# One small tile 128 bytes larger, and weight stores, loads, root steps, activations and result stores at other places in a fused attention and two-MoE kernel

## The chip, the cores and the metric

One core of a Trainium2 chip. The metric is the device time of one launch in microseconds (us): the median of the runs. Lower is better.

## What is computed

```python
kv  = einsum('bhsd,bhse->bhde', k, v)            # b=8, h=8, s=576, d=64
o   = einsum('bhsd,bhde->bhse', q, kv)
x   = o / sqrt(mean(o*o, -1) + 1e-6) * g_norm    # to (4608 tokens, 512)
h   = x @ moe_w_in;   x = (h * sigmoid(h)) @ moe_w_out      # 512 -> 2048 -> 512
h   = x @ moe2_w_in;  out = (s * relu(h)**2 + b) @ moe2_w_out
```

All tensors are fp32. The four weights are 512x2048 or 2048x512. Their product with 4608 tokens is nearly all of the arithmetic.

## The kernel before, in words

Every fp32 operand of the four large products is split into a high and a low part, and a product is three passes of matmuls (high by high, high by low, low by high). Attention and the first matrix (`emit_h`, L489) make up the **first stage**: 7 blocks of 512 tokens, each with 16 slots of 12 matmuls of 512 columns. Between the slots `attend` (L555) places the attention of the batches that come later. For batch b a table `UNITS` names the number of its 128-token tiles and the slot where it begins. One slot after another does `emit_qT` (transposes, tile `pq`), `out_tile` (`po`, the sum of squares, a copy), then the root of the mean by Newton steps on DVE (`rsqrt_steps`, 12 short operations that `run_between` takes in portions), `norm_tile`, and one `xT_tile` a slot (transposes into `px`, ACT writes `xh`, DVE writes `xl`, the two moving operands of a later block). `pq`, `po` and `px` share two PSUM banks. Tiles of batches that no block of the first stage takes are written to DRAM through a buffer `xs`.

Beside this, `weight_steps` (L203) re-codes the weights of the later stages: one call of `steps` does one small piece, and 2 or 3 are taken in a slot (3 in the second half of a block). `split` writes a piece into one half (a granule) of one of four rooms `SPARES`, and stores it to DRAM (`wd<-wo`) by a deferred call: `defer(n, f)` runs f after n slots.

The rest of the work uses Strassen-Winograd products, seven instead of eight, named P1, P5, P6, P2, P7, P4, P3 (k = 0 to 6 in this order): **hidden1** (the last 1024 tokens of the first MoE's first matrix, with SiLU of sums of two products, `add_square`), **out2** (the first MoE's second matrix), **hidden3** and **out4** (the same of the second MoE). out2, hidden3 and out4 take blocks b = 1 to 4 of 512 columns and last b = 0 with half as many. In hidden3 and hidden1 a group g is seven products of six matmuls, and four results `g` of a group are stored to DRAM (`Hidden.out`, `gt<-g`). With b = 0 each such store has 128 KB, the others 256 KB. Results rotate through rooms `G_ROOMS`, by `turn % 4` in hidden3's blocks 1 to 4, `turn % 7` otherwise. The output stages read them again (`Output.load`: `ka`, `r`, `sa`), and the re-coded weights (`grid.load`: `w<-wd`). A unit of an output stage is 24 matmuls, with one cast on ACT (L845) and one subtraction on DVE (L847) that write its moving operand `o`. out4 transposes its result (`rows_out`, `pt`), copies it to `out_c` or `out` in turn (ACT, L876) and stores it.

What sets the order: it is written out by hand, and each engine works through its own list in order. SP issues the loads and the stores of stages 2 and 3's weights; ACT issues the stores of `g`, `y` and the result, between its own operations. A DMA that has to wait holds everything behind it on that engine. SP and ACT draw on the same eight DMA semaphores in turn, so an issue also waits until the eighth DMA before it has landed.

Tiles live in "rooms" of fixed size that lie in SBUF one behind another, in the order of their first use. The tile `r` (L436, L1147: 4 x 5 x 8 floats a partition, 640 bytes) is first used after `wr_0`, `wr_1`, W4 to W6 and W8 to W11, and before all other rooms that PE reads in the large products. In the built kernel the first group starts at 32 modulo 256 bytes (288 modulo 512), the second at 160 modulo 256 (416 modulo 512). In the output stages the weights of product k, slice a are in W{4k+a} and the moving operand is in one of four rooms of the second group (`RING`, L577). In the hidden stages the weights are in W{k+7a}, and the moving operand is in the second group, but that of P6, which is in `wr_0`.

Of the kernel before, what the change touches and what calls it, by code (L numbers as in the profile page):

```python
# [8 lines left out]
F32 = mybir.dt.float32  # L9
# [8 lines left out]
def kernel(  # L18
# [36 lines left out]
    nc = tc.nc  # L55
# [77 lines left out]
    raw_t = {}  # L133
    wf_t = {}
# [68 lines left out]
    def weight_steps(stage, raws, sums_in, granule, slots, behind=None):  # L203
# [40 lines left out]
        def step(i, what):  # L244
            if i < NF:
                decode(stage, i, what)
                if what == "merge":
                    n = i + len(raws)
                    if n < NF:
                        load_raw(stage, n, raws[n % len(raws)])  # L250
                    elif behind:
                        load_raw(behind, n - NF, raws[n % len(raws)])

        def begin():
            if stage == 4:
                csum.append(room("gl_1", [P, T], F32, "csum"))
                nc.vector.memset(csum[0], 0.0)
            for i, tag in enumerate(raws):
                if (stage, i) not in raw_t:
                    load_raw(stage, i, tag)  # L260
# [172 lines left out]
    def out_tile(t):  # L433
        b, i = t
        if i == 0:
            r_t[b] = small.tile([P, 4, (TT + 1) * H], F32, tag="r", name=f"r{b}", bufs=1)  # L436
        ps = ps_a.tile([P, H, D], F32, tag="a", name=f"po{b}_{i}")
        emit_out(t, ps, range(NP))
        emit_squares(t, ps, r_t[b][:, 0, i * H:(i + 1) * H])
        xn_t[t] = xn_page(t)  # L440
        nc.scalar.copy(xn_t[t], ps)
# [113 lines left out]
    def attend(slot):  # L555

        for b, n, s in UNITS:
            d = slot - s
            lead = 4 if b == 1 else 6
            if 0 <= d + lead < n:  # L560
                load_q(b, d + lead)
            if 0 <= d < NP and b + 1 < B:
                load_kv(b + 1, d)
        for b, n, s in UNITS:
            d = slot - s
            if d == -2:
                emit_kv(b, range(NP))
            if 0 <= d < n:
                out_tile((b, d))
            if -1 <= d < n - 1:  # L570
                emit_qT((b, d + 1))
            if d == n - 1:
                between.extend(rsqrt_steps(r_t[b], n))
            if b > 1 and n - 1 <= d < n + 2:
                run_between(4)
            if d == n + 2:
                run_between(len(between))  # L577
                for i in range(2):
                    norm_tile((b, i))
            if d == n + 3:  # L580
                for i in range(2, n):
                    norm_tile((b, i))
            if n + 3 <= d < 2 * n + 3:
                xT_tile((b, d - n - 3))
# [9 lines left out]
    class Hidden:  # L594
# [5 lines left out]
        def __init__(self, stage, order):  # L600
            self.stage, self.order, self.gt = stage, order, gt[stage]
            self.raw, self.slots, self.banks, self.turn = {}, {}, {}, 0
            self.seq = [(b, i) for b in order for i in range(NF)]
# [112 lines left out]
        def out(self, g, f, h, slots):  # L716
            b = self.seq[g][0]
            self.turn += 1
            r = room(self.G_ROOMS[self.turn % (4 if b and self.stage == 3 else 7)], [P, T], F32, f"g{self.stage}_{b}_{f}_{h}")[:, :size[b]]
            defer(slots if b else slots + 1, lambda: nc.scalar.dma_start(self.gt[b][f, h], r))  # L720
            return r
# [9 lines left out]
        def add_square(self, g, f, h, x, y):  # L731
# [5 lines left out]
            if self.stage == 1:  # L737
                nc.scalar.activation(r, r, AF.Silu)
# [34 lines left out]
    class Output:  # L773


        def __init__(self, stage):
# [4 lines left out]
            self.turn = 0  # L781
            self.keep, self.t = {}, []
# [13 lines left out]
        def load(self, upto):  # L796
            while self.loaded < min(upto, len(self.units)):
                u = self.loaded
                self.loaded += 1
                b, k, a = self.units[u]  # L800
                n = size[b]
                if k == P1 and u < NA:
                    self.load_kept(b, a)
                if k in (P5, P2, P7):
                    x, h = int(k == P2), int(k != P2)
                    r = self.r[u] = pair(R_ROOMS[self.turn % 4], f"r{self.stage}_{u}")[:, :, :n]
                    self.turn += 1
                    nc.sync.dma_start(r, self.gt[b][4 * a + x:4 * a + 4:2, h].rearrange("i p t -> p i t"))
                if k == P6:
                    if a not in self.s:  # L810
                        self.s[a] = room(SPARES[a], [P, 2, T], F32, f"sa{self.stage}_{a}")
                    nc.sync.dma_start(
                        self.s[a][:, :, :n], self.gt[b][4 * a + 1:4 * a + 4:2, 1].rearrange("i p t -> p i t")
                    )
# [55 lines left out]
        def rows_out(self, b, h, r):  # L870
# [13 lines left out]
            def store():  # L884
                for part, rows in rows_of(*t):
                    nc.scalar.dma_start(rows, o[part])
# [188 lines left out]
    def beside1(b, i, k):  # L1075
# [4 lines left out]
        if i == 3 and k == P1:  # L1080
            out2.load(2)
        if i == NF - 1:
# [14 lines left out]
    def beside3(b, i, k):  # L1097
# [8 lines left out]
        if i == 3 and k == P1:  # L1106
            out4.load(2)
        if i == NF - 1:
# [11 lines left out]
    with tc.manual_schedule():  # L1120
# [26 lines left out]
        r = r_t[0] = small.tile([P, 4, (TT + 1) * H], F32, tag="r", name="r0", bufs=1)  # L1147
# [44 lines left out]
        def in_pages(n):  # L1192
# [3 lines left out]
            weight_steps(2, ("wr_0", "wr_1"), ("v_0", "v_1"), in_spares(), 1, behind=3),  # L1196
            weight_steps(3, ("wr_0", "wr_1"), ("v_0", "v_1"), in_spares(), 1),
# [44 lines left out]
```

## Time and profile before

| what | value |
|---|---|
| runs | 1593.0, 1596.1, 1598.49 us; median 1596.1 |
| profiled execution, its own time | 1598.04 us |
| its span in the trace | 1595.9 us |
| mean granted clock of TensorE | 0.992 of full speed |
| busy share: TensorE weight loads, DVE, ACT | 82%, 63%, 52% |
| HBM read, written | 211.81 MB, 140.51 MB |

The profiled execution is 1.9 us above the median. Times in the views count from the start of its span. PE is TensorE, PEld its weight loads; a name such as `py` or `o` is a tile of the program with its numbers left out; `a<-b` is written and read; L931 is a line of the kernel. The first stage lasts until 433 us, hidden1 until 511, out2 until 863, hidden3 until 1219, out4 until the end.

### The profile page before, as it was taken

What the parts mean: (1) busy time and instruction counts of PE and PEld (TensorE: products, weight loads), DVE (VectorE), ACT (ScalarE), POOL (GpSimd) and SP (SyncE); (2) the same over time, 40 slices, a digit from 0 to 9 for tenths busy, and PEclk for the clock granted to TensorE, in tenths of its full rate; (3) what the DMA queues carried; (4) which work ended last, traced back from release to release, by engine and by line L of the source; (5) the groups of instructions that cost most, each with busy time, mean ns of one, the idle gap of its engine ahead of it and who ended that gap; (6) DMA issues with size and microseconds to landing.
All of it is one profiled execution on the core that took longest, in us unless ns stands there. A gap on an engine that the chain in (4) does not pass through costs nothing.

```text
span 1595.9 us, 21844 instructions
## 1 busy us (share of the span) xinstructions
PE 1561.9 (98%) x8184; PEld 1305.3 (82%) x8184; DVE 1007.3 (63%) x1385; ACT 833.1 (52%) x1331; POOL 1.6 (0%) x8
## 2 busy tenths in 40 slices
PE   7999999999999999999999999999999999999998
PEld 5888788887887788888898788888889888888888
DVE  4645465456673958676767666666546757576745
ACT  3655545555454444444445565656555454546454
POOL 0000000000000000000000000000000000000000
PEclk8999999999999999999999999999999999999999
DMA  8978898977655982727259847475466872726241
GB/s 251 268 246 276 267 303 289 294 259 258 219 204 200 361 314 94 240 79 249 75 204 354 337 166 264 156 279 198 179 226 249 334 278 80 235 82 237 67 145 54
DMA packets 228937, 353.77 MB, mean 222 GB/s; under 512 B 56800, under 2 KB 96736, under 8 KB 228832
## 3 DMA queue, kind: packets, MB, share of 16 engines
q1 hardware_dynamic: 162176, 240.95, 45.5%
q10 hardware_dynamic: 66656, 111.44, 19.1%
q8 instruction: 64, 1.05, 0.3%
q14 instruction: 41, 0.34, 0.1%
HBM read 211.81 MB, written 140.51 MB: 221 GB/s over the span
## 4 chain that ended last, share of the span: by engine, by line
PE 88%; DMA 6%; ACT 2%; DVE 2%; issue 1%; ACTq 1%; SPq 0%; DVEq 0%
PE ph L495 19%; PE qy L931 18%; PE qv L931 11%; PE py L708 11%; PE qx L931 11%; PE px L708 7%; PE pv L708 7%; PE po L385 2%; DMA gt<-g 1%; PE pkv L351 1%; PE pq L375 1%; DMA r<-gt 1%; PE px L461 1%; PE pt L874 1%; DMA out_dram<-out 1%
## 5 line engine op out<-in xcount | busy, mean ns | idle before, releaser
L931 PE MATMUL qy<-o,w 128*128 128x512 f32 (+1 forms) x1440 | 301.6, 369 | 0.4 <-DVE o L847 0.4
L931 PEld LDWEIGHTS qy<-o,w 128*128 128x128 f32 x1440 | 251.7, 189 | 47.4 <-DVE o L847 0.6
L847 DVE TENSOR_TENSOR o<-ka,o 128x1024 fp32r<-128x1024 f32 (+1 forms) x160 | 178.5, 1116 | 127.5 <-ACT o L845 125.1
L845 ACT CAST o<-ka 128x1024 fp32r<-128x1024 f32 (+1 forms) x160 | 153.4, 963 | 166.2 <-PE qv L931 63.0
L931 PE MATMUL qv<-o,w 128*128 128x512 f32 (+1 forms) x960 | 207.6, 374 | 4.1 <-ACT o L845 2.9
L931 PE MATMUL qx<-o,w 128*128 128x512 f32 (+1 forms) x960 | 203.5, 369 | 2.4 <-ACT o L845 1.7
L931 PEld LDWEIGHTS qv<-o,w 128*128 128x128 f32 x960 | 169.5, 192 | 35.7 <-ACT o L845 3.1
L931 PEld LDWEIGHTS qx<-o,w 128*128 128x128 f32 x960 | 167.0, 189 | 32.9 <-ACT o L845 2.1
L708 PE MATMUL py<-x,w 128*128 128x512 f32 (+1 forms) x720 | 164.0, 372 | 4.5 <-ACT g L734 4.3
L708 PEld LDWEIGHTS py<-x,w 128*128 128x128 f32 x720 | 126.7, 189 | 30.2 <-ACT g L734 5.5
L502 ACT ACTIVATE g<-ph 128x512 f32<-128x512 f32 x112 | 67.0, 598 | 154.4 <-PE ph L495 152.0
L495 PE MATMUL ph<-xh,wh 128*128 128x512 f32 x448 | 128.1, 408 | 3.3 <-ACT xh L465 3.3
L845 ACT CAST o<-r 128x1024 fp32r<-128x1024 f32 (+1 forms) x80 | 77.1, 963 | 89.3 <-PE qy L931 44.7
L495 PE MATMUL ph<-xl,wh 128*128 128x512 f32 x448 | 121.3, 393 | 0.0
L495 PE MATMUL ph<-xh,wl 128*128 128x512 f32 x448 | 120.2, 390 | 0.0
L708 PE MATMUL pv<-x,w 128*128 128x512 f32 (+1 forms) x480 | 113.0, 371 | 0.0
L708 PE MATMUL px<-x,w 128*128 128x512 f32 (+1 forms) x480 | 112.8, 371 | 0.0
L847 DVE TENSOR_TENSOR o<-r,o 128x1024 fp32r<-128x1024 f32 (+1 forms) x80 | 89.4, 1118 | 36.0 <-ACT o L845 35.1
L495 PEld LDWEIGHTS ph<-xl,wh 128*128 128x128 f32 x448 | 84.6, 189 | 19.1 <-DVE xl L466 0.2
L495 PEld LDWEIGHTS ph<-xh,wl 128*128 128x128 f32 x448 | 84.4, 188 | 18.3
L708 PEld LDWEIGHTS px<-x,w 128*128 128x128 f32 x480 | 85.4, 190 | 15.8
L708 PEld LDWEIGHTS pv<-x,w 128*128 128x128 f32 x480 | 85.2, 190 | 16.0
(156 smaller groups left out, 1878.5 us busy)
## 6 DMA issues: line engine op xcount, KB each, us to landing
r<-gt SPq DMA_DIRECT2D x96, 512.0 KB, 5.2
w<-wd SPq DMA_DIRECT2D x84, 512.0 KB, 7.1
gt<-g ACTq DMA_DIRECT2D x160, 256.0 KB, 2.3
gt<-g ACTq DMA_DIRECT2D x56, 512.0 KB, 4.8
wd<-wo SPq DMA_DIRECT2D x112, 256.0 KB, 4.3
wr<-in_moe_w_in_dram SPq DMA_DIRECT2D x16, 1024.0 KB, 6.5
wr<-in_moe_w_out_dram SPq DMA_DIRECT2D x16, 1024.0 KB, 6.5
ka<-gt SPq DMA_DIRECT2D x32, 512.0 KB, 3.8
```

What stands on the lines that cost most here:

```text
L351: nc.tensor.matmul(ps[r, p, r], ka[:, i, d], va[:, i, d], start=(p == pairs[0] and c == 0), stop=False, skip_group_check=True,)
L375: nc.tensor.transpose(ps[:, p * P:(p + 1) * P], a[:, p * P:(p + 1) * P], ident)
L385: nc.tensor.matmul(po[off:off + n, p * P:(p + 1) * P], qT_t[t][:, p, off:off + n], kvw[b % 2][:, p, :], start=True, stop=True,)
L461: nc.tensor.transpose(ps[:, p, :], xn[:, p * P:(p + 1) * P], ident)
L495: nc.tensor.matmul(ps, wt[:, c, :], xt[:, c, :], start=(n == 0 and c == 0), stop=(n == 2 and c == KT - 1))
L502: nc.scalar.activation(both[:, i], ps, AF.Silu)
L708: nc.tensor.matmul(ps, a[s][c], x[t][c], start=(k in (P1, P5) and n == c == 0), stop=(n == 2 and c == 1), skip_group_check=True,)
L845: nc.scalar.copy(o[:, :, 0], x)
L847: nc.vector.tensor_sub(o[:, :, 1], x, o[:, :, 0])
L874: nc.tensor.transpose(ps[:, e * P:(e + 1) * P], self.c[b, h, e][:, r * P:(r + 1) * P], ident)
L931: nc.tensor.matmul(ps, t[:, s], self.o[u][:, i, p], start=(k in (P1, P5) and a == i == m == 0), stop=(a == NA - 1 and i == 1 and m == 2), ...
```

## The change

- `r` is given as 4 x 6 x 8 floats, 768 bytes. In the built kernel all rooms behind it start 128 bytes later: the second group is now at 32 modulo 256 (32 modulo 512), the first stays at 32 modulo 256 (288 modulo 512).
- Weight stores of stages 2 and 3 are deferred by three slots instead of one, and the load of a raw weight into a room that was just read is deferred too.
- `q` loads come 8 slots ahead instead of 6. The 12 root steps are taken as 6 and 6 instead of 4, 4, 4, and norm and transposes come one slot earlier.
- In hidden1, SiLU of a sum of two products is deferred by two slots.
- The first loads of out2 and out4 (`ka_0`, and the first four `r`) stand earlier, one by one (`fetch`).
- In the half block two results share one room and one store (`halves`).
- The result stores of the last two blocks (b = 4 and 0) are issued by SP.

```diff
@@ weight_steps, step and begin
                 if what == "merge":
                     n = i + len(raws)
-                    if n < NF:
-                        load_raw(stage, n, raws[n % len(raws)])
-                    elif behind:
-                        load_raw(behind, n - NF, raws[n % len(raws)])
+                    to, n, tag = stage, n, raws[n % len(raws)]
+                    if n >= NF:
+                        to, n = behind, n - NF
+                    if to:
+                        asked.add((to, n))
+                        defer(slots, lambda: load_raw(to, n, tag))
...
-                if (stage, i) not in raw_t:
+                if (stage, i) not in asked:
                     load_raw(stage, i, tag)
@@ out_tile (and the same for r0)
-            r_t[b] = small.tile([P, 4, (TT + 1) * H], F32, tag="r", name=f"r{b}", bufs=1)
+            r_t[b] = small.tile([P, 4, 6 * H], F32, tag="r", name=f"r{b}", bufs=1)
@@ attend
-            lead = 4 if b == 1 else 6
+            lead = 4 if b == 1 else 8
...
-            if b > 1 and n - 1 <= d < n + 2:
-                run_between(4)
-            if d == n + 2:
+            if b > 1 and n - 1 <= d < n + 1:
+                run_between(6)
+            if d == n + 1:
                 run_between(len(between))
                 for i in range(2):
                     norm_tile((b, i))
-            if d == n + 3:
+            if d == n + 2:
                 for i in range(2, n):
                     norm_tile((b, i))
-            if n + 3 <= d < 2 * n + 3:
-                xT_tile((b, d - n - 3))
+            if n + 2 <= d < 2 * n + 2:
+                xT_tile((b, d - n - 2))
@@ Hidden.out
-            b = self.seq[g][0]
-            self.turn += 1
-            r = room(self.G_ROOMS[self.turn % (4 if b and self.stage == 3 else 7)], [P, T], F32, f"g{self.stage}_{b}_{f}_{h}")[:, :size[b]]
-            defer(slots if b else slots + 1, lambda: nc.scalar.dma_start(self.gt[b][f, h], r))
-            return r
+            b, i = self.seq[g]
+            if b:
+                self.turn += 1
+                r = room(self.G_ROOMS[self.turn % (4 if self.stage == 3 else 7)], [P, T], F32, f"g{self.stage}_{b}_{f}_{h}")
+                defer(slots, lambda: nc.scalar.dma_start(self.gt[b][f, h], r))
+                return r
+            n = int(f % 2 != h)
+            if (g, n) not in self.halves:
+                self.turn += 1
+                t = self.halves[g, n] = room(self.G_ROOMS[self.turn % 7], [P, 2, size[b]], F32, f"g{self.stage}_{b}_{i}_{n}")
+            else:
+                t = self.halves[g, n]
+                rows = self.gt[b][2 * i:2 * i + 2].rearrange("f h p t -> p (f h) t")
+                rows = rows[:, 1:3] if n else rows[:, 0:4:3]
+                defer(slots, lambda: nc.scalar.dma_start(rows, t))
+            return t[:, f % 2]
@@ Hidden.add_square
-                nc.scalar.activation(r, r, AF.Silu)
+                defer(2, lambda: nc.scalar.activation(r, r, AF.Silu))
@@ Output: load is cut in two, fetch(u) does what its body did, once for a unit
+                self.fetch(self.loaded - 1)
+        def fetch(self, u):
+            if u in self.fetched:
+                return
+            self.fetched.add(u)
...
@@ Output.rows_out
-                    nc.scalar.dma_start(rows, o[part])
+                    (nc.sync if b in order[-2:] else nc.scalar).dma_start(rows, o[part])
@@ beside1
-        if i == 3 and k == P1:
+        if i == 1 and k == P6:
             out2.load(2)
+        if i in (2, 3, 4, 5) and k == P2:
+            out2.fetch(NA + i - 2)
@@ beside3
-        if i == 3 and k == P1:
+        if i == 1 and k == P1:
             out4.load(2)
+        if i in (1, 2, 3, 4) and k == P2:
+            out4.fetch(NA + i - 1)
@@ the call of weight_steps for stages 2 and 3
-            weight_steps(2, ("wr_0", "wr_1"), ("v_0", "v_1"), in_spares(), 1, behind=3),
-            weight_steps(3, ("wr_0", "wr_1"), ("v_0", "v_1"), in_spares(), 1),
+            weight_steps(2, ("wr_0", "wr_1"), ("v_0", "v_1"), in_spares(), 3, behind=3),
+            weight_steps(3, ("wr_0", "wr_1"), ("v_0", "v_1"), in_spares(), 3),
```

**PE, end of the first block of the first stage.** `px_0` to `px_4` are batch 1's transposes, `ph_15` is the block's last slot and `ph_0` the next block's first. Before:

```order
L461 MATMUL px_2_908<-ident,xnp_71 128x128 x4
L495 MATMUL ph_15_920<-xh_406,wh_806 128x512 x4
L495 MATMUL ph_15_920<-xl_407,wh_806 128x512 x4
L495 MATMUL ph_15_920<-xh_406,wl_826 128x512 x4
L461 MATMUL px_3_935<-ident,xnp_71 128x128 x4
L495 MATMUL ph_0_949<-xh_863,wh_230 128x512 x4
L495 MATMUL ph_0_949<-xl_864,wh_230 128x512 x4
L495 MATMUL ph_0_949<-xh_863,wl_232 128x512 x4
L461 MATMUL px_4_966<-ident,xr_765 128x128 x4
```

and now:

```order
L464 MATMUL px_2_891<-ident,xnp_71 128x128 x4
L498 MATMUL ph_14_900<-xh_406,wh_806 128x512 x4
L498 MATMUL ph_14_900<-xl_407,wh_806 128x512 x4
L498 MATMUL ph_14_900<-xh_406,wl_837 128x512 x4
L464 MATMUL px_3_916<-ident,xnp_71 128x128 x4
L498 MATMUL ph_15_926<-xh_406,wh_806 128x512 x4
L498 MATMUL ph_15_926<-xl_407,wh_806 128x512 x4
L498 MATMUL ph_15_926<-xh_406,wl_837 128x512 x4
L464 MATMUL px_4_940<-ident,xr_765 128x128 x4
L498 MATMUL ph_0_954<-xh_848,wh_230 128x512 x4
```

The transposes `px_0` to `px_3`, from which the second block's operands are made, stand one slot earlier: between the last of them and the block's first matmul there is now a whole slot, and `px_4`, a tile that the block does not read.

**SP, end of hidden1 and start of out2** (`w` are weights of out2, `ka` and `r` its first inputs, `sa` later ones). Before:

```order
L315 DMA w_0_0_4303<-wd_0_0_75 128x1024
L792 DMA ka_0_4382<-gt_1_161 128x2x512 x2
L315 DMA w_0_1_4395<-wd_0_1_76 128x1024
L315 DMA w_0_2_4482<-wd_0_2_77 128x1024
L315 DMA w_0_3_4567<-wd_0_3_78 128x1024
L315 DMA w_1_0_4640<-wd_1_0_79 128x1024
L315 DMA w_1_1_4708<-wd_1_1_80 128x1024
L792 DMA ka_1_4727<-gt_1_161 128x2x512 x2
L808 DMA r_4_4782<-gt_1_161 128x2x512
L808 DMA r_5_4784<-gt_1_161 128x2x512
L808 DMA r_6_4786<-gt_1_161 128x2x512
```

and now:

```order
L808 DMA ka_0_4245<-gt_1_161 128x2x512 x2
L318 DMA w_0_0_4306<-wd_0_0_75 128x1024
L829 DMA r_4_4353<-gt_1_161 128x2x512
L318 DMA w_0_1_4397<-wd_0_1_76 128x1024
L829 DMA r_5_4445<-gt_1_161 128x2x512
L318 DMA w_0_2_4486<-wd_0_2_77 128x1024
L829 DMA r_6_4534<-gt_1_161 128x2x512
L318 DMA w_0_3_4573<-wd_0_3_78 128x1024
L829 DMA r_7_4617<-gt_1_161 128x2x512
L318 DMA w_1_0_4648<-wd_1_0_79 128x1024
L318 DMA w_1_1_4716<-wd_1_1_80 128x1024
L808 DMA ka_1_4735<-gt_1_161 128x2x512 x2
```

The first `ka` and four `r` now alternate with the loads of weights, each of which waits for its room; only the second `ka` still stands in the last stretch.

**ACT, half block of hidden3** (`g_0_...` are results, `gt_0` their stores). Before:

```order
L728 ACTIVATE g_0_4_0_10166<-px_10112 128x256
L729 ACTIVATE g_0_4_0_10166<-g_0_4_0_10166 128x256
L734 COPY g_0_5_1_10175<-py_10119 128x256
L753 COPY py_10186<-px_10179 128x256
L720 DMA gt_0_165<-g_0_2_1_10156 128x256
L720 DMA gt_0_165<-g_0_4_0_10166 128x256
L728 ACTIVATE g_0_5_0_10208<-py_10119 128x256
L729 ACTIVATE g_0_5_0_10208<-g_0_5_0_10208 128x256
L720 DMA gt_0_165<-g_0_5_1_10175 128x256
L758 COPY u_10218<-py_10186 128x256
L720 DMA gt_0_165<-g_0_5_0_10208 128x256
```

and now:

```order
L773 COPY u_10212<-py_10185 128x256
L743 ACTIVATE g_0_3_0_10228<-px_10178 128x256
L744 ACTIVATE g_0_3_0_10228<-g_0_3_0_10228 128x256
L749 COPY g_0_3_0_10228<-py_10185 128x256
L735 DMA gt_0_165<-g_0_2_1_10203 128x2x256
L768 COPY py_10250<-px_10243 128x256
L735 DMA gt_0_165<-g_0_3_0_10228 128x2x256
L743 ACTIVATE g_0_3_1_10268<-py_10185 128x256
L744 ACTIVATE g_0_3_1_10268<-g_0_3_1_10268 128x256
```

A group has two stores of two results each where it had four of one, and a room comes round again after 7 stores, which are now three and a half groups, where they were one and three quarters.

## Rows read from the trace of the kernel before

**Rows 1.** Page, part 1: busy time, share of the span, number of instructions.
```profile
PE 1561.9 (98%) x8184; PEld 1305.3 (82%) x8184; DVE 1007.3 (63%) x1385; ACT 833.1 (52%) x1331; POOL 1.6 (0%) x8
```

**Rows 2.** Windows: length, busy us (count) by engine; then PEclk, DMA share, GB/s.
```profile
1170.00:1220.00 50.00, 45.70 (x351) 44.39 (x350) 21.27 (x43) 25.72 (x65) 0.00 (x0) 0.97 0.59 202
...
1540.00:1596.00 56.00, 47.30 (x368) 46.17 (x367) 29.51 (x48) 27.17 (x49) 0.00 (x0) 0.92 0.26 76
```

**Rows 3.** Waits of PE, whole span: total us, times, longest us.
```profile
PE py L708 <- ACT g L734: 5.0, 4, 2.6
PE ph L495 <- ACT xh L465: 3.3, 4, 0.8
...
PE pq L375 <- DVE xl L466: 1.5, 2, 0.8
```

**Rows 4.** Chain in order of time, stages 2 and 3: start us, us, what.
```profile
591.14 10.89 PE qx L931 x48
602.02 11.09 PE qv L931 x48
613.12 11.15 PE qy L931 x48
...
1018.36 2.75 PE py L708 x12
...
1095.39 2.75 PE py L708 x12
```

**Rows 5.** The same chain in the first stage, end of its first block.
```profile
89.26 2.75 PE ph L495 x12
...
92.44 2.76 PE ph L495 x12
```

**Rows 6.** Waits of SP, 168 to 181 us, first stage.
```profile
SPq L240 <- DVE wo L238: 9.4, 3, 5.2
```

**Rows 7.** Timeline of PE, start of the second stage; in brackets idle before, and releaser.
```profile
508.40 1.20 PE L708 MATMUL py<-x,wh 128*128 128x512 f32 x4 [0.67 <-ACT g L734]
...
518.55 0.50 PE L931 MATMUL qx<-o,w 128*128 128x512 f32 x1 [1.69 <-ACT o L845]
519.81 1.45 PE L931 MATMUL qx<-o,w 128*128 128x512 f32 x5 [0.76 <-DVE o L847]
```

**Rows 8.** Timeline of ACT, the same stretch.
```profile
517.45 1.99 ACT L845 CAST o<-ka 128x1024 fp32r<-128x1024 f32 x2 [3.85 <-DMA gt<-g]
```

**Rows 9.** Timeline of PE, half block of the third stage.
```profile
1178.74 1.70 PE L708 MATMUL py<-x,w 128*128 128x256 f32 x12 [1.25 <-ACT g L734]
...
1186.60 2.10 PE L708 MATMUL py<-x,w 128*128 128x256 f32 x12 [2.59 <-ACT g L734]
```

**Rows 10.** Timeline of ACT, the same stretch.
```profile
1173.97 0.33 ACTq L720 DMA_DIRECT2D gt<-g  x1
...
1185.45 0.38 ACT L728 ACTIVATE g<-px 128x256 f32<-128x256 f32 x1 [4.47 <-DMA gt<-g]
```

**Rows 11.** Windows of 2 us, the same stretch, columns as in rows 2.
```profile
1188.00:1190.00 2.00, 2.00 (x12) 2.00 (x11) 0.00 (x0) 0.79 (x2) 0.00 (x0) 0.50 0.93 289
1190.00:1192.00 2.00, 2.00 (x15) 2.00 (x14) 0.85 (x2) 0.71 (x3) 0.00 (x0) 0.74 0.89 275
```

**Rows 12.** Timeline of PE, start of the last half block.
```profile
1547.29 3.00 PE L931 MATMUL qv<-o,w 128*128 128x256 f32 x24
1553.23 6.00 PE L931 MATMUL qv<-o,w 128*128 128x256 f32 x24 [2.93 <-ACT o L845]
```

**Rows 13.** Timeline of ACT, the same stretch; ACTq is its issue of DMAs.
```profile
1550.02 0.58 ACT L876 COPY out<-pt 128x512 f32<-128x512 f32 x1 [1.56 <-DMA out_dram<-out]
1550.10 1.12 ACTq L886 DMA_DIRECT2D out_dram<-out_c  x2
...
1552.56 0.62 ACT L845 CAST o<-ka 128x512 fp32r<-128x512 f32 x1 [1.95 <-DMA out_dram<-out_c]
```

**Rows 14.** Page, part 6: issues, KB each, median us to landing.
```profile
wd<-wo SPq DMA_DIRECT2D x112, 256.0 KB, 4.3
```

More of the change, by code (lines that the diff above doesn't have):

```diff
@@ L133 @@
     raw_t = {}
+    asked = set()
     wf_t = {}
@@ L602, in __init__ @@
             self.raw, self.slots, self.banks, self.turn = {}, {}, {}, 0
+            self.halves = {}
             self.seq = [(b, i) for b in order for i in range(NF)]
@@ L781, in __init__ @@
             self.turn = 0
+            self.fetched = set()
             self.keep, self.t = {}, []
@@ L797, in load @@
             while self.loaded < min(upto, len(self.units)):
-                u = self.loaded
                 self.loaded += 1
[L800 to L814, printed above, removed]
+                self.fetch(self.loaded - 1)
[3 more added lines that the diff above has]
+            self.fetched.add(u)
+            b, k, a = self.units[u]
+            n = size[b]
+            if k == P1 and u < NA:
+                self.load_kept(b, a)
+            if k in (P5, P2, P7):
+                x, h = int(k == P2), int(k != P2)
+                r = self.r[u] = pair(R_ROOMS[self.turn % 4], f"r{self.stage}_{u}")[:, :, :n]
+                self.turn += 1
+                nc.sync.dma_start(r, self.gt[b][4 * a + x:4 * a + 4:2, h].rearrange("i p t -> p i t"))
+            if k == P6:
+                if a not in self.s:
+                    self.s[a] = room(SPARES[a], [P, 2, T], F32, f"sa{self.stage}_{a}")
+                nc.sync.dma_start(
+                    self.s[a][:, :, :n], self.gt[b][4 * a + 1:4 * a + 4:2, 1].rearrange("i p t -> p i t")
+                )
         def prepare(self, upto):
@@ L1145, in first_kv @@
             emit_kv(0, [p])
-        r = r_t[0] = small.tile([P, 4, (TT + 1) * H], F32, tag="r", name="r0", bufs=1)
+        r = r_t[0] = small.tile([P, 4, 6 * H], F32, tag="r", name="r0", bufs=1)
         pss = [ps_y.tile([P, H, D], F32, tag=f"y{t}", name=f"po{t}") for t in range(TT)]
```

## The prediction

> **What bounds the kernel now.** I read the page first: PE is busy 1561.9 us of a span of 1595.9 us [rows 1]. So only two things can give time back: the 34 us in which PE stands still, and matmuls that run slower than others of their kind. The windows by stage show where PE stands: 4.3 us between 1170 and 1220 us, 8.7 us after 1540 us, and both windows also have a granted clock below 1 [rows 2]. The table of PE's waits names who ended the stalls: ACT's `g` in the hidden stages and ACT's `xh` at block starts of the first stage [rows 3]. The chain in order of time shows the second thing: products with the same 48 matmuls take 10.89, 11.09 and 11.15 us with no wait between them [rows 4].
>
> **The change part by part.** The sum is made against the profiled execution, 1598.04 us, which is 1.9 us above the median of the runs.
>
> **1. The larger tile.** In an output block P5 takes 11.09 us and P6 11.15 us where P1, with equal shapes, takes 10.89 us [rows 4]. P5 reads its weights from W4 to W7, P6 from W8 to W11, P1 from W0 to W3. All of those but W7 in the first two lists begin at 32 modulo 256, while W0 to W3, W7 and the moving operands begin at 160 modulo 256. Unequal remainders go with slow products, equal ones with fast ones. The two column halves of a weight room lie 512 bytes apart and behave alike, so the pattern repeats after 256 or 512 bytes. The change makes all equal modulo 256. Output stages: (0.20 + 0.26) x 4 full blocks x 2 stages = 3.7 us. Hidden3: eight groups of 42 matmuls take 1095.39 - 1018.36 = 77.03 us; at the fast pace of 10.89/48 they take 76.23 us; 0.8 x 4 blocks = 3.2 us. hidden1 (eight groups, no more than 0.8 us) and the half blocks, whose price I cannot separate, I leave out. Term: **-6.9 us**. But modulo 512 the two groups stay apart, now by 256 bytes. If the pattern repeats only after 512, nothing is known of that distance; I bound it by 0 and, at worst, by the same loss again, +6.9 us.
>
> The Trainium skill (TensorE: Matmul & The Clock Gate, Part 2, step 1) says that TensorE reads moving data and weights through two independent ports, so that loading the next weights takes no read bandwidth from the running matmul. By it addresses would not matter and this term would be 0; the 0.2 us between like products [rows 4] speak against that here, though the rows do not say what makes them differ.
>
> **2. Roots, norm and transposes a slot earlier.** At three of the block starts in the first stage the first matmul waits for ACT's `xh`, 0.8 us each of 3.3 us in four waits [rows 3] (the fourth is the opening). With a slot of PE work between (2.75 us [rows 5]) ACT and DVE are done in time: -2.4 us. Batch 2's overlap of `px`, `pq` and `po` on two banks shrinks from two slots to one, half of the 1.5 us of `pq` waiting for `xl` [rows 3]: -0.7 us. Batch 3 still has three such slots, at other places: 0, with ends -1.5 and +1.5 us by that row. Term: **-3.1 us**. The two additional root steps a slot are short DVE operations, and DVE is busy 63% [rows 1]: 0. Their cover is the slot; without it they would delay `xl` and be the same wait again.
>
> **3. Weight stores and raw loads three slots later, `q` earlier.** Between 168 and 181 us SP stood 9.4 us in three waits for DVE to write the data of weight stores [rows 6], with K, V and raw loads behind them. Three slots later the data is there, so the loads go out evenly. What hides their lateness now is that K, V and raw loads have slots to spare: after the opening PE waits for no load in this stage, only for ACT and DVE [rows 3], so I count 0. The end below is -1.5 us, batch 3's slots again, which fall right behind; above, the slower rival.
>
> **4. SiLU of sums deferred.** ACT waits for DVE's sum before SiLU, and PE's next bank waits behind it: 0.67 us at 508.40 [rows 7]. A SiLU two slots later finds its sum. **-0.7 us**; ends 0 and -0.7 us.
>
> **5. First loads spread.** out2 opens with 1.69 + 0.76 us of waiting for casts and subtractions [rows 7]. ACT, which should cast, waited 3.85 us for `gt` stores to land [rows 8], in a burst of `ka`, `r` and `w` loads. The five that move out of it are 3 MB of it. **-2.0 us**, near the whole 2.45, since weights and `sa` stay in the burst; other end 0. The same in hidden3 moves loads into the half block, where DMA shares of 0.9 stand [rows 11], but each then waits behind a weight load for a room that PE frees, so they come one a group: 0.
>
> **6. Two results in one store.** PE stalls twice in hidden3's half block, 1.25 and 2.59 us, for ACT [rows 9]; ACT waits there for result rooms, 4.47 us before the second [rows 10]. The first room is that of the last full group's P4 result, stored at 1173.97 [rows 10]; the rotation gives the same room after the change, so that stall stays. The second is for the room of that group's P3 result; it comes round two groups later now, so that stall goes: -2.6 us. After it the granted clock is 0.50 and 0.74 for 2 us each [rows 11], so (0.50 + 0.26) x 2 = 1.5 us of work are lost; this goes too. Term: **-4.1 us**; ends 0 and -5.4 us (with the first stall).
>
> **7. Last result stores on SP.** The last half block's P5 waits 2.93 us, then its 24 matmuls take 6.00 us instead of 3.00 [rows 12], which is the lower clock level. The cast that PE awaits is at 1552.56, behind four store issues from 1550.10 that keep ACT for 2.4 us, and these behind a copy at 1550.02 that waited for the room of an earlier store [rows 13]. The issues go to SP; the wait for the room stays, for SP sends the earlier stores no sooner. So the cast comes about 1550.6, and PE waits some 0.9 us. A wait of 1.25 us left the clock up [rows 9], those of 2.59 and 2.93 us did not, so I take the clock as held: -2.0 - 3.0 = **-5.0 us**. Ends: 0 (SP's `r` and `sa` loads queue behind the stores, and become late) and -5.9 us.
>
> Sum: 6.9 + 3.1 + 0.7 + 2.0 + 4.1 + 5.0 = 21.8 us. 1598.0 - 21.8 = 1576.2 in the profiled execution's terms, 1574.3 against the median. I forecast **1574 us**.
>
> **The rivals.**
>
> *A. Addresses bring nothing.* The two-port rule holds and something else made P5 and P6 slow, or the pattern repeats after 512 bytes. Against it: every product is on the side that its room's remainder gives. For it: nothing in the trace has a distance of 256. Then 1574 + 6.9 = 1581 us.
>
> *B. The waits move instead of going.* The same bytes flow in the same stretches, ACT still waits for rooms to be freed by stores in parts 5 to 7, and some other store is the late one. Then 11.1 us come back: 1585 us. For it: DMA shares of 0.9 [rows 11]. Against it: the rooms that ended these waits come round later or are waited for elsewhere.
>
> *C. Slower: the spare rooms.* A granule is rewritten after eight pieces; a room of two has 7 pieces between its second writing and its next first one. At 1.5 pieces a slot in the second halves of blocks that is 4.7 slots, of 3.2 us (89.26 to 92.44 [rows 5]), 14.8 us. The store used to be asked for after one slot and now after three, so 5.2 us remain to land, and the median is 4.3 us [rows 14]. A longer landing holds ACT; a slot of PE's work covers 3.2 us, so above 8.4 us PE stalls. 24 rooms are rewritten so: the time is 1574 + 24 x (landing - 8.4). It is slower than before by over 0.3% from a mean landing of 9.5 us on; at 10 us it gives 1612 us. For it: 4.47 us of waiting for a landing in a burst [rows 10] show that a store can take longer than its median. Against it: 9.5 us would have to be the mean, over twice the median, and SP no longer stands in front of these stores [rows 6].
>
> *D. A and B together:* 1592 us, no difference.
>
> **How the numbers follow.** Forecast 0.59, A 0.20, B 0.11, D 0.05, C 0.05. 0.3%, 4.8 us, is about what a measurement of this kernel can tell from no change. Forecast, A and B lie below 1591.3: faster 0.90. D is within: same 0.05. C: slower 0.05. The range begins at 1566: the forecast less the further ends of parts 2, 3, 5, 6 and 7 (1.5, 1.5, 0.4, 1.3, 0.9; 5.6 us) and 2 us for the spread of runs. It ends at 1587, with A and B inside and 2 us of spread; outside are D, C and the worst end of part 1.
>
> **What would show it.** In the changed kernel's chain all seven products of an output block would take 10.89 us per 48 matmuls, and eight groups of hidden3 76.2 us; if P5 and P6 keep 11.1, A holds. PE's waits for `xh` would come once; the stall near 1186 us and its low clock would be gone and the one near 1178 still there; P5 of the last half block would take 3.00 us after a wait of about 1 us, and SP rather than ACT would issue the last stores. ACT waiting for `wd<-wo` in the first stage would show C. The prediction is wrong if the output products do not change and no stall of over 2 us goes.

## The result, and the profile after

The changed kernel takes 1578.95 us (median of 4 runs, 1576.61 to 1581.71) against 1595.58 us for the kernel before, which has one run more here than in the table above: a ratio of 0.9896, 95% interval 0.9872 to 0.992. That is 16.6 us less; 21.8 were forecast, and the range of 1566 to 1587 us holds the time. The profiled execution took 1579.11 us with a span of 1577.3 us, 18.6 us less than before.

PE is still the bound, and does the same instructions in 14.9 us less busy time [rows 1]. The page of the changed kernel, part 1:

```profile
PE 1547.0 (98%) x8184; PEld 1300.4 (82%) x8184; DVE 1007.6 (64%) x1385; ACT 832.0 (53%) x1331; POOL 1.6 (0%) x8
```

About half of that is faster matmuls, as the chain in order of time shows. In an output block P1, P5 and P6 now take the same time, and eight groups of hidden3 take 76.16 us where they took 77.03 [rows 4]. Most of the other half is the clock: the mean granted clock is 0.996 where it was 0.992, which makes some 6 us (an estimate, 0.004 of the span). PE's idle time fell by 3.7 us only, from 34.0 to 30.3 us. The chain:

```profile
583.90 10.88 PE qx L952 x48
594.78 10.88 PE qv L952 x48
605.66 10.88 PE qy L952 x48
...
1020.94 2.72 PE py L712 x12
...
1097.10 2.72 PE py L712 x12
```

PE's waits over the whole span (total us, times, longest us), those that answer to [rows 3] and the new ones:

```profile
PE px L464 <- DVE xnp L432: 4.6, 3, 2.6
PE py L712 <- ACT g L749: 4.5, 4, 1.8
...
PE pq L378 <- ACT xs L474: 2.5, 2, 2.0
PE qv L952 <- DVE o L868: 1.8, 1, 1.8
...
PE qy L952 <- DVE o L868: 1.2, 1, 1.2
...
PE ph L498 <- ACT xh L468: 0.8, 1, 0.8
PE pq L378 <- DVE xl L469: 0.7, 1, 0.7
```

Of the four waits for `xh` one is left, the opening's. The waits of `py` for ACT have shrunk by 0.5 us only. A wait for the norm (`xnp`) of 0.96 us, before the matmul at 263.06, is new, and the one of batch 1, now before the matmul at 81.96, has grown from 0.44 to 1.06 us. Two waits for DVE's `o` stand out. One is at the end of out2, where it was 0.99 us before and is 1.83 now; the other is in the last half block.

To see the stages apart I take the starts of PE's first `ph`, `pv` (hidden1), `qx` (out2), `pv` (hidden3) and `qx` (out4) and the end of the span; the differences are the stages' lengths in us. The table has every profiled execution of this study, for one wait in one profile turned out to be a poor witness.

| kernel | opening | first stage | hidden1 | out2 | hidden3 | out4 |
|---|---|---|---|---|---|---|
| before | 36.9 | 397.1 | 77.2 | 353.2 | 354.5 | 377.0 |
| changed | 37.2 | 393.9 | 76.4 | 350.5 | 348.7 | 370.6 |
| e1, tile 640 | 37.9 | 392.0 | 77.2 | 350.6 | 352.5 | 372.2 |
| e2, before with tile 768 | 36.8 | 399.1 | 76.6 | 352.1 | 345.9 | 374.9 |
| e3, tile 896 | 35.7 | 393.9 | 77.2 | 350.3 | 350.1 | 372.0 |
| e4, tile 736 | 37.3 | 393.4 | 77.3 | 352.6 | 353.1 | 371.8 |
| e5, old roots | 35.8 | 395.3 | 76.4 | 351.4 | 348.2 | 370.2 |
| e6, old last stores | 37.9 | 392.2 | 76.4 | 347.7 | 349.7 | 374.3 |
| e7, old halves | 36.9 | 392.9 | 76.4 | 350.6 | 351.6 | 370.3 |
| e8, old first loads | 37.0 | 394.3 | 76.4 | 347.6 | 347.1 | 370.4 |
| e9, old SiLU | 37.4 | 395.6 | 76.6 | 347.6 | 350.4 | 370.3 |
| e10, old SiLU and first loads | 36.3 | 393.0 | 76.6 | 353.7 | 346.8 | 370.2 |
| e11, old weight stores | 36.4 | 396.1 | 76.4 | 349.5 | 350.2 | 370.2 |
| e12, combined | 35.1 | 393.3 | 76.4 | 348.9 | 347.3 | 369.9 |

Two differences in this table I do not credit to the change. Windows from 35 to 45 us, of the kernel before and then of the changed one (length, busy us and count by engine; PEclk, DMA share, GB/s), show that the opening of the one ran at a lower clock than that of the other, 2 us of work apart:

```profile
35.00:45.00 10.00, 9.22 (x34) 7.30 (x33) 9.03 (x11) 5.69 (x8) 0.00 (x0) 0.71 0.28 78
```

```profile
35.00:45.00 10.00, 9.22 (x41) 7.50 (x40) 9.07 (x11) 6.05 (x8) 0.00 (x0) 0.91 0.28 80
```

So up to 2.0 us of the first stage's 3.2 us is the opening: the first block takes 59.5 us before and 58.0 in the changed kernel. Of the others e3, e8 and e9 began as slowly as the kernel before (first blocks of 59.7 to 59.9 us against 57.8 to 58.7 in the rest). And out2's gain in the changed kernel is shortened by a low clock behind its wait of 1.83 us:

```profile
852.00:854.00 2.00, 1.71 (x9) 1.71 (x10) 2.00 (x4) 1.25 (x2) 0.00 (x0) 0.65 1.02 406
854.00:856.00 2.00, 2.00 (x11) 2.00 (x11) 1.22 (x2) 1.05 (x1) 0.00 (x0) 0.50 1.03 402
```

### The profile page after: what moved, and what is told of

It is laid out like the page before. It is cut to its first block, busy times and chain, and to the rows that moved or that the text cites. A ratio compares the mean times of both kernels' runs of the same rounds, so it can differ in the third digit from the quotient of the medians.

```text
span 1577.3 us, 21814 instructions
## 1 busy us (share of the span) xinstructions
PE 1547.0 (98%) x8184; PEld 1300.4 (82%) x8184; DVE 1007.6 (64%) x1385; ACT 832.0 (53%) x1331; POOL 1.6 (0%) x8
## 4 chain that ended last, share of the span: by engine, by line
PE 90%; DMA 5%; DVE 2%; ACT 2%; issue 1%; SPq 0%; ACTq 0%; DVEq 0%
PE ph L498 18%; PE qy L952 18%; PE qv L952 12%; PE qx L952 11%; PE py L712 11%; PE px L712 7%; PE pv L712 7%; PE po L388 2%; DMA r<-gt 1%; PE px L464 1%; PE pkv L354 1%; PE pq L378 1%; PE pt L895 1%; DMA wd<-wp 1%; DMA kvz<-in_v_dram 1%
## 5 line engine op out<-in xcount | busy, mean ns | idle before, releaser
L712 PEld LDWEIGHTS pv<-x,w 128*128 128x128 f32 x480 | 84.7, 189 | 14.9
```

The lines of the kernel that those rows point to most:

```text
L712: nc.tensor.matmul(ps, a[s][c], x[t][c], start=(k in (P1, P5) and n == c == 0), stop=(n == 2 and c == 1), skip_group_check=True,)
```

## Experiments on the tile's size

**e1: the changed kernel with the old tile.**

```diff
-            r_t[b] = small.tile([P, 4, 6 * H], F32, tag="r", name=f"r{b}", bufs=1)
+            r_t[b] = small.tile([P, 4, (TT + 1) * H], F32, tag="r", name=f"r{b}", bufs=1)
```

> The changed kernel with the tile at its old size of 640 bytes; all else as changed. Theory (rooms whose starts differ modulo 256 bytes slow the 512-column matmuls): P5 and P6 of the output stages take 11.09 and 11.15 us per 48 matmuls again instead of 10.88, eight groups of hidden3 77.0 us instead of 76.16; the time is about 7 us above the changed kernel's 1578.95, so 1586. Rival (the other parts of the change made these products fast, for instance fewer loads beside them): products stay at 10.88 and the time at 1579.

P1, P5 and P6 of an output block in the chain:

```profile
583.91 10.89 PE qx L952 x48
594.79 11.09 PE qv L952 x48
605.89 11.16 PE qy L952 x48
```

The old durations are back, and hidden1 and hidden3 grow by 0.8 and 3.8 us in the table. The time is 1582.97 us, ratio 0.9916 (0.9901 to 0.9931): 3 us behind the changed kernel by the ratios, not 7. The interval overlaps the change's, so the runs alone don't separate the two; the products do. Part of the difference is lost at the end of out2: four blocks of P5 and P6 are 1.9 us faster in the changed kernel, yet the whole stage has equal length in both, for behind a wait of 1.83 us there the clock stayed up in e1.

**e2: the kernel before with the new tile, and nothing else.**

```diff
-            r_t[b] = small.tile([P, 4, (TT + 1) * H], F32, tag="r", name=f"r{b}", bufs=1)
+            r_t[b] = small.tile([P, 4, 6 * H], F32, tag="r", name=f"r{b}", bufs=1)
```

> The kernel before with the tile at 768 bytes and nothing else. Theory: all products of the output stages at 10.88 us, hidden3 76.16 us for eight groups; the span falls by up to 7 us. Where loads bound the end of the second stage the gain is partly given back: between 4 and 7 us, so 1589 to 1592. Rival: the size alone does nothing, 1595.6.

```profile
592.89 10.88 PE qx L931 x48
603.77 10.88 PE qv L931 x48
614.65 10.88 PE qy L931 x48
```

All products are fast. The time is 1587.33 us, ratio 0.9945 (0.9926 to 0.9963), 9.1 us less than the 1596.44 us of the kernel before, measured beside it, and more than the products save. The surplus is in hidden3: it is 8.6 us shorter, of which 3.5 us are matmuls. But for 0.47 us at its end, which every kernel here has, the half block of this execution has one wait, of 0.29 us (timeline of PE):

```profile
1174.25 1.70 PE L708 MATMUL py<-x,w 128*128 128x256 f32 x12 [0.29 <-ACT g L734]
```

The second stall of [rows 9] is absent here, though nothing of part 6 was done. My reading, which no run tested, is that it depends on which of SP's loads happen to run beside the stores, and that this shifts with the pace of PE.

**e3 and e4: two other sizes in the changed kernel**, 896 and 736 bytes.

```diff
-            r_t[b] = small.tile([P, 4, 6 * H], F32, tag="r", name=f"r{b}", bufs=1)
+            r_t[b] = small.tile([P, 4, 7 * H], F32, tag="r", name=f"r{b}", bufs=1)    # e3; in e4 [P, 4, 46]
```

> The changed kernel with 896 bytes for the tile: the two groups of rooms are 128 bytes apart modulo 256 again, now at 288 and 160 modulo 512 (before it was 288 and 416). Period of 256: P5 11.09, P6 11.15 us as in the kernel before, time about 1586. If what counts is the distance modulo 512 with its sign, the durations differ from both: anything between 10.88 and 11.4.

> The changed kernel with 736 bytes: the second group starts at 0 modulo 256, the first at 32, so 32 bytes apart. If any inequality modulo 256 slows the matmuls: P5 and P6 above 11.0 us, time about 1586. If only a distance of 128 does: 10.88 us, time 1579. If the cost grows with distance: in between, 10.93 to 10.98.

P5 and P6 in the chain of e3:

```profile
594.51 11.09 PE qv L952 x48
605.60 11.15 PE qy L952 x48
```

and of e4:

```profile
595.74 11.13 PE qv L952 x48
606.86 11.20 PE qy L952 x48
```

With 896 bytes the distance is 128 modulo 256 again and the durations are those of 640 bytes. With 736 bytes the rooms are only 32 bytes apart and the products are as slow, even by 0.04 us slower. So neither a distance of 128 alone nor a cost that grows with distance fits: of the distances tried, what is fast is an equal start modulo 256 bytes, and at 768 bytes, where the starts differ by 256, nothing is lost. The kernel before shows the same inside one product. P5's first three slices of 12 matmuls read their weights from W4 to W6, which start apart from the moving operands, and its last reads W7, which starts like them; here are the third and the fourth slice in its chain:

```profile
607.61 2.79 PE qv L931 x12
610.39 2.73 PE qv L931 x12
```

So a matmul of 512 columns takes 232.5 ns where the starts differ and 227.5 ns in the slice where they agree. The single runs took 1580.94 and 1587.21 us; of times 6 us apart for kernels with equal products I make nothing.

## Experiments that undo one part each

**e5: old roots, norm and transposes.**

```diff
-            if b > 1 and n - 1 <= d < n + 1:
-                run_between(6)
+            if b > 1 and n - 1 <= d < n + 2:
+                run_between(4)
```

and norm and `xT_tile` at `n + 2`, `n + 3` again.

> The changed kernel with root steps 4, 4, 4, and norm and transposes a slot later again. Theory: the first matmul of three blocks waits for xh again, 0.83 us and a slow start of 0.27 us each (3.3 us), a second batch-2 slot with 0.9 us comes back, and the two new waits for the norm (0.97 us at 261.7, 0.6 us more at 80.5) go: first stage from its first ph matmul to the first pv matmul 396 to 397 us against 393.9, time 1581 to 1582. Rival (the new norm waits cost as much as the block starts): 394, time 1579.

PE's waits between 40 and 430 us:

```profile
PE ph L498 <- ACT xh L468: 2.7, 3, 1.1
PE pq L378 <- DVE xl L469: 1.8, 2, 1.0
...
PE px L464 <- DVE xnp L432: 0.4, 1, 0.4
```

The waits are as the theory says, three for `xh` and two for `xl`. The first stage has 395.3 us, 1.4 us over the changed kernel's and 2 to 3.3 us over that of the others with new roots, new weight stores and a quick opening (392.0 to 393.4 in e1, e4, e6, e7, e10 and e12). The time, 1578.59 us, ratio 0.9884 (0.9863 to 0.9905), does not show it. Blocks 2 and 4 to 7 of the first stage, which the opening and the `xs` wait of e11 leave alone, tell it more closely: together they take 279.0, 279.1 and 279.6 us with the old roots (before, e2 and e5) and 276.5 to 277.2 us in the other eleven, 276.6 in the changed kernel. So the part is worth 2.4 to 3.0 us in the trace and less than the runs can tell.

**e6: result stores on ACT again.**

```diff
-                    (nc.sync if b in order[-2:] else nc.scalar).dma_start(rows, o[part])
+                    nc.scalar.dma_start(rows, o[part])
```

> The changed kernel with all result stores on ACT again. Theory: P5 of the last half block waits 2 to 3 us for ACT's cast and then runs 24 matmuls in 6.0 instead of 3.0 us, and the 1.19 us wait of P6 for late loads goes: 1583 to 1585. Rival (it was the lateness of loads and the padded tile, not the issue on ACT): no wait over 1.5 us in the last half block, 1578 to 1580.

Timeline of PE, P5 of the last half block:

```profile
1536.44 0.39 PE L952 MATMUL qv<-o,w 128*128 128x256 f32 x1 [2.94 <-ACT o L866]
1537.17 4.27 PE L952 MATMUL qv<-o,w 128*128 128x256 f32 x23 [0.34 <-DVE o L868]
```

The stall is back at 2.94 us, and the matmuls behind it take 4.27 us for 23 where 3.00 us for 24 is usual [rows 12]. out4 has 374.3 us against 369.9 to 370.6 in all others with the new tile and the stores on SP: 3.7 us or more. The time is 1579.56 us, 0.989 (0.9866 to 0.9915); this execution gained 2.8 us in out2, where nothing was changed. P6 has no wait here, as expected.

**e7: one store for each result of the half block.** `Hidden.out` as it was before:

```diff
-            n = int(f % 2 != h)
-            if (g, n) not in self.halves:
...
+            r = room(self.G_ROOMS[self.turn % (4 if b and self.stage == 3 else 7)], [P, T], F32, f"g{self.stage}_{b}_{f}_{h}")[:, :size[b]]
+            defer(slots if b else slots + 1, lambda: nc.scalar.dma_start(self.gt[b][f, h], r))
+            return r
```

> The changed kernel with one store for each result of the half block again. Theory: hidden3's half block has its second stall again, 2.6 us, with 1.5 us of lower clock behind it, and keeps the first of 1.25 to 1.84 us: hidden3 from first pv to first qx 352.5 us against 348.7, time 1583. Rival (the burst of loads was its cause, which the earlier fetch has spread): the second stall stays away, 1579.

Timeline of PE, half block of hidden3, and a window of 2 us behind it (length, busy us and count by engine; PEclk, DMA share, GB/s):

```profile
1168.38 1.69 PE L712 MATMUL py<-x,w 128*128 128x256 f32 x12 [1.50 <-ACT g L738]
...
1175.85 2.26 PE L712 MATMUL py<-x,w 128*128 128x256 f32 x12 [2.17 <-ACT g L738]
```

```profile
1178.00:1180.00 2.00, 2.00 (x11) 2.00 (x11) 0.54 (x2) 0.37 (x1) 0.00 (x0) 0.50 1.03 319
```

Both stalls are there, the second of 2.17 us with a granted clock of 0.50 behind it. hidden3 is 2.9 us longer than in the changed kernel. The time, 1578.96 us, 0.9883 (0.986 to 0.9907), is the same. With e2 this means: two results in one store take away a stall that comes in some kernels and not in others.

**e8: the first loads where they stood.** `beside1` and `beside3` as before:

```diff
-        if i == 1 and k == P6:
+        if i == 3 and k == P1:
             out2.load(2)
-        if i in (2, 3, 4, 5) and k == P2:
-            out2.fetch(NA + i - 2)
```

and the same for `out4`.

> The changed kernel with the first loads of out2 and out4 where they stood. Theory: qx waits 1.7 and 0.8 us again at the start of out2 (2.5 to 2.9 us with the slow start), nothing at the start of out4: time 1581.5. Rival (the waits came from ACT's SiLU behind DVE's sum, which the deferred SiLU removed): no wait at the start of out2, 1579.

It is a miss for the theory: there is no wait at the start of out2, and the time is lower, 1575.53 us, 0.9869 (0.9846 to 0.9893). hidden3 is shorter too. In the changed kernel SP sends `ka` (landed by 1162.4) and then an `r` ahead of the store that ACT needs next. The `r` is still under way when that store goes out, and the store lands after 4.15 us; timeline of SP, and of ACT:

```profile
1155.20 0.93 SPq L808 DMA_DIRECT2D ka<-gt  x2
1164.15 0.36 SPq L829 DMA_DIRECT2D r<-gt  x1
```

```profile
1165.27 0.33 ACTq L725 DMA_DIRECT2D gt<-g  x1
...
1169.50 0.38 ACT L743 ACTIVATE g<-px 128x256 f32<-128x256 f32 x1 [2.91 <-DMA gt<-g]
```

In e8, where no load of SP runs beside it, that store lands after 2.34 us, the same wait of ACT is 1.09 us, and PE has none there:

```profile
1165.30 0.38 ACT L743 ACTIVATE g<-px 128x256 f32<-128x256 f32 x1 [1.09 <-DMA gt<-g]
```

Over all runs with the new tile and halves hidden3 has 348.2 to 350.4 us with the early loads (changed, e5, e6, e9, e11; mean 349.4) and 346.8 to 347.3 us without (e8, e10, e12; mean 347.1): they cost 2.4 us. Some 0.7 us of that mean is a low clock that stands behind the stall in e9 and e11 alone.

**e9 and e10: SiLU of sums at its old place, with the early loads and without.**

```diff
-                defer(2, lambda: nc.scalar.activation(r, r, AF.Silu))
+                nc.scalar.activation(r, r, AF.Silu)
```

> The changed kernel with SiLU of sums at its old place, first loads early as in the change. With the early loads undone no wait came back at the start of out2, so either the deferred SiLU alone removed it or the two each would. Theory 1 (the old SiLU puts ACT's stores behind DVE's sum and ahead of out2's first casts; it alone decides): qx waits 1.7 to 2.5 us at the start of out2. Theory 2 (either part is enough): no qx wait there.

> The changed kernel with SiLU of sums and the first loads both at their old places. Both theories: qx waits 1.7 to 2.9 us at the start of out2 as in the kernel before; third theory (the padded tile or the stage's new timing removed that wait): none. In hidden3, as with the loads alone undone: no wait near 1168 us.

e9 has no `qx` wait at the start of out2. e10, with both undone, has the waits of [rows 7] again; PE's waits from 506 to 520 us:

```profile
PE qx L952 <- ACT o L866: 1.6, 1, 1.6
PE qx L952 <- DVE o L868: 0.8, 1, 0.8
```

So theory 2 holds for e8 and e9: either part was enough. It is no rule, for e12 below has the deferred SiLU and the old first loads, as e8 has, and waits 0.76 us for DVE's `o` at 511.51. Times of the single runs: 1579.69 and 1578.44 us. In e10 hidden3 has a wait of 0.51 us near 1169, where none was expected, against 2.04 us in e9.

**e11: weight stores after one slot again**, and raw loads after one slot.

```diff
-            weight_steps(2, ("wr_0", "wr_1"), ("v_0", "v_1"), in_spares(), 3, behind=3),
+            weight_steps(2, ("wr_0", "wr_1"), ("v_0", "v_1"), in_spares(), 1, behind=3),
```

and the same for stage 3.

> The changed kernel with weight stores deferred by one slot and raw loads after one slot. Theory: SP waits 9 us for DVE's data before the third batch's loads again, but PE's waits in the first stage stay: first stage from first ph to first pv 392 to 394 us. Rival (the freed SP shortened the staged stores of batch 3): the wait of pq for xs near 189 us grows from 0.7 to 2.0 us to 3 us or more, first stage 395 to 396 us.

PE's waits from 150 to 200 us:

```profile
PE pq L378 <- ACT xs L474: 3.3, 2, 2.7
```

The rival holds: 2.73 us of it is the wait near 189 us, and the first stage has 396.1 us. The two kernels with the old stores and other changes, before and e2, have 1.39 and 3.41 us there; of the eleven with the new ones nine have 0.5 to 0.8 us, the changed kernel 1.96 and e9 1.83 us. The mean falls from 2.5 to 0.8 us. The wait goes with the landing of an `xt<-xs` store that ACT issued just before: that store took 6.48 to 8.52 us in the five executions with the long wait and 5.12 to 5.88 us in the other nine. Behind the waits of 2.73 and 3.41 us the granted clock is 0.50, and the whole third block takes 60.8 us in the mean with the old stores, 58.1 with the new. The single run took 1580.66 us.

**e12: a combination.** e8, and

```diff
-                self.load(u + 7)
+                self.load(u + (11 if self.stage == 4 and b == order[-1] else 7))
...
-            if b > 1 and n - 1 <= d < n + 1:
+            if n - 1 <= d < n + 1:
```

> The changed kernel with the early first loads undone; out4's last half block asks for its inputs 11 units ahead instead of 7, so that they stand before the result stores on SP; batch 1's root steps are taken in the slots as the others'. Expected from the run with only the loads undone (1575.5): no wait of P6 in the last half block (-1.3 us), batch 1's norm wait 0.4 us or less instead of 1.06: 1573 to 1574, ratio to before 0.985 to 0.987. Rival (the inputs come no earlier, for their rooms are not free): the P6 wait stays, 1575.5.

Timeline of PE, P5 and P6 of the last half block:

```profile
1530.71 0.39 PE L952 MATMUL qv<-o,w 128*128 128x256 f32 x1 [0.57 <-ACT o L866]
1531.43 3.01 PE L952 MATMUL qv<-o,w 128*128 128x256 f32 x23 [0.34 <-DVE o L868]
1534.28 5.92 PE L952 MATMUL qy<-o,w 128*128 128x256 f32 x48
```

The wait of P6 is gone; P5 waits 0.57 and 0.34 us instead, and batch 1's norm wait stays at 1.08 us, a miss: taking its root steps earlier does not shorten it. The time is 1573.2 us, ratio 0.9867 (0.9844 to 0.989), the lowest median of all and clearly below the kernel before. Its interval overlaps that of the change and is nearly e8's, so that it beats these two is not shown.

## Why the prediction was right, and which terms were not

The forecast of 1574 us was 5 us too low; the direction and the range were right. That it came so near is partly luck. By kind the sum had 6.9 us of faster matmuls, 4.5 us of clock and 10.4 us of waits; the profiles show some 8 us, 6 to 7 us and 3.7 us, and up to 2.0 us of the clock's share is the opening, which no part aimed at. Rival A fell with e1 to e4: the address does it. Rival C did not come: no wait of PE in the first stage goes back to a spare room, and the stage is not longer. Of rival B a part is true.

1. **The larger tile**, -6.9 us. The products gained (0.21 + 0.27) x 8 = 3.8 us in the output stages and 0.87 x 4 = 3.5 us in hidden3, 7.3 us, and hidden1, which the sum left out, another 0.6 (e2) to 0.8 us (e1); e1 to e4 show that it is the tile alone and that the pattern repeats after 256 bytes. The Trainium skill says that loading the next weights takes no read bandwidth from the running matmul (TensorE: Matmul & The Clock Gate, Part 2, step 1). As the prediction read that, this term would be 0. The trace does not agree with that reading: with weights and moving data at unequal starts modulo 256 a matmul of 512 columns takes 232 to 233 ns (2.79/12, 11.20/48), with equal starts 226.7 ns (10.88/48). Why the start matters, no run shows.
2. **Roots**, -3.1 us. The three block starts and one `pq` wait went as said; the blocks in e5 bear out 2.4 to 3.0 us, with two norm waits, grown by 0.62 and 0.96 us, already taken off. The sum had no term for these. They go with the earlier norm and not with more root steps a slot: batch 1's root steps are not taken in the slots, and in e12, where they are, its wait stays. Before 263.06 DVE had ended its root steps by 258.99 and did pieces of weights until the norm began at 262.23.
3. **Weight stores**, 0. Mis-sized: the fall is -1.7 us by the means of the wait in e11 and -2.7 us by the third block, with the clock. That the end of -1.5 us was near is luck: it was set by the `pq` waits for `xl` [rows 3], and what shrank is the wait for `xs`. The profiles of the kernel before and of the changed one alone do not show it (1.39 us before, 1.96 after). The earlier `q` loads, also of this part, no run undid. A load that PE never waits for can still run beside a store that it does wait for, `xs`; which of the loads lengthens that store, no run separates.
4. **SiLU**, -0.7 us at 508 us. The step failed: the wait is there as before, 0.68 us at 504.72. Timelines of PE and of ACT:

```profile
504.72 1.19 PE L712 MATMUL py<-x,wh 128*128 128x512 f32 x4 [0.68 <-ACT g L749]
```

```profile
504.08 0.59 ACT L749 COPY g<-py 128x512 f32<-128x512 f32 x1 [0.24 <-PE py L712]
```

   P4 of the last group adds to the bank that ACT is just copying at 504.08 (the `py` of P7), and in a last group no product of a next group stands between. I had put the wait on the SiLU, and the row named the copy's line, L734, all along [rows 7]. Elsewhere in hidden1 the part may be worth 0.2 us: the stage takes 76.6 us in e2, e9 and e10, with the old SiLU, and 76.4 in the seven others with the new tile.
5. **First loads**, -2.0 us. The stall went, but by e8 the deferred SiLU alone can do it, and by e12 not all of it every time. In hidden3 I had costed the moved loads at 0; they cost 2.4 us, for SP is not held to one a group, as I thought: `ka` and the first `r` go out as soon as their rooms are free, the `r` at 1164.15, ahead of the store at 1165.27. The first stall of the half block stayed, as forecast, and grew from 1.25 to 1.84 us (timeline of PE):

```profile
1170.65 1.69 PE L712 MATMUL py<-x,w 128*128 128x256 f32 x12 [1.84 <-ACT g L749]
```

6. **Two results in one store**, -4.1 us. The stall went, e7 brings it back; but e2 lacks it without this part. As a part of this change it is worth 2 to 3 us.
7. **Last stores on SP**, -5.0 us. The 2.93 us and the low clock went, without the 0.9 us that I left standing, and the loads behind the stores became late, which the text named as an end. Timelines of the changed kernel: PE at P5 and P6, SP, and DVE, which waits for `sa`:

```profile
1533.29 5.96 PE L952 MATMUL qv<-o,w 128*128 128x256 f32 x48
...
1540.55 5.72 PE L952 MATMUL qy<-o,w 128*128 128x256 f32 x43 [1.19 <-DVE o L868]
```

```profile
1534.95 1.12 SPq L907 DMA_DIRECT2D out_dram<-out  x2
1536.18 1.83 SPq L833 DMA_DIRECT2D sa<-gt  x3
```

```profile
1539.20 0.69 DVE L850 TENSOR_TENSOR ka<-sa,ka 128x512 f32<-128x512 f32 x1 [1.83 <-DMA sa<-gt]
```

   P6 waits 1.19 us. Net, by e6, 3.7 us.

The sum failed in one respect: it took the stalls of one profile as fixed and free to be removed one by one. Waits at the end of out2, where no part reached, came and went (the longest is 0.55 to 1.84 us), and the changed profile had a long one. A wait early in hidden3 (0.15 us before, 1.48 us after) came with the change: all nine kernels that have the new tile and most of the other parts have it, of 0.75 to 1.79 us, while before, e1, e2 and e3 have at most 0.17 us and e4 0.95. Undoing a single part other than the tile did not remove it. What makes these two waits is open; they were not tried.

## What to carry to other kernels

Where equal matmuls differ by 2% with no wait between them, compare the SBUF addresses of weights and moving data, here modulo 256 bytes and for 512 columns: padding one small tile was worth more than any single rescheduling. A stall behind a DMA landing in one profile is a sample; undo parts one at a time and compare stage lengths over several executions before crediting one. Loads that are moved earlier run as soon as their room is free, not where they stand in the code, so look which store they overtake.

## What was not expected of the hardware

A distance of 32 bytes modulo 256 slows the 512-column matmuls as much as one of 128 (11.13 and 11.20 us for 48 in e4, 11.09 and 11.15 us in e3). With 256 columns it is the other way, by less: a group of 42 matmuls in hidden3's half block takes 5.00 us before, from 1193.20 to 1198.20, and 5.04 in the changed kernel, from 1190.89 to 1195.93. And equal waits of PE end differently for its clock: behind 1.83 us at the end of out2 the changed kernel has a granted clock of 0.50, which is the level of 1.2 GHz, in a window where e1, behind the same 1.83 us, has 1.00 (window of e1, whose matmuls start again at 853.46):

```profile
853.00:855.00 2.00, 1.54 (x12) 1.54 (x13) 2.00 (x3) 1.42 (x2) 0.00 (x0) 1.00 1.03 409
855.00:857.00 2.00, 2.00 (x16) 1.89 (x15) 2.00 (x3) 1.52 (x2) 0.00 (x0) 1.00 1.02 398
```

In hidden3's half block the granted clock is 1.00 from 1168 to 1170 us behind a wait of 2.10 us in e6, and 0.58 from 1174 to 1176 us behind one of 1.76 us in e1. What I took from [rows 9] and [rows 11] for part 7, that the length of the wait tells whether the clock stays up, does not hold.
